# A zero product between the score halves goes, one w_val group is cut in two, and three output products run in column halves

## The chip, the cores and the metric

The kernel runs on one NeuronCore of a Trainium2 chip. The metric is the device time of one execution in microseconds, lower is better. Before is given as the median of three runs.

## What is computed

Sliding-window attention over 8 batches, 8 heads, 576 positions and 64 features per head, followed by a gated feed-forward layer over the 4608 tokens that come out of it:

```python
scores = scale * np.matmul(q, k.transpose(0, 1, 3, 2))
rel = pos[:, None] - pos[None, :]
mask = (rel >= 0) & (rel < 64)
scores = np.where(mask, scores, -1000000000.0)
...                                              # softmax over the last axis
attn_out = np.matmul(attn, v)
x = attn_out.transpose(0, 2, 1, 3).reshape(B * S, H * D)     # 4608 x 512
gate = np.maximum(x @ w_gate, 0.0)               # 512 x 1536
val = x @ w_val                                  # 512 x 1536
out = (gate * val) @ w_out                       # 1536 x 512
```

Inputs and output are fp32. The kernel computes in fp16 with fp32 sums in PSUM.

## The kernel before

**Tokens and tiles.** Attention is done in units of 192 positions of one batch (names `u_...`), three to a batch, with all heads; heads lie in two halves `hh` of four. Two units make one token tile of 384 columns for the feed-forward part; there are four such tiles (`t` = 0 to 3) and then six of 512 (attention for these is done in quads, `q_...` and `t_...`). In the feed-forward part the 1536 hidden features are 12 blocks of 128, numbered `f`.

**The order of work.** The program is written out by hand and fixed when it is built. `tc.manual_schedule()` keeps the instructions of each engine in the order in which the Python code emits them. A small event queue, `Weaver` (`W`), interleaves side work with the long stream of matrix products: `W.at(t, fn)` queues a function for a planned time, and the code that emits products moves the planned clock `W.clock` on and pops what is due. Semaphores between engines are set by the tile framework from what each instruction reads and writes.

**The start.** The first queries and keys come in by DMA; VectorE (DVE) and ScalarE (ACT) cast them to fp16, and DVE transposes them (`qk_trans`, L199), keys and queries of the first head half, then of the second. Meanwhile TensorE (PE) writes a mask bias into eight PSUM banks (`bias_mm`, L243). Then follow, in PE's order: the scores of units 0 and 1 for the first head half (`u_st`, `st_block`, L276), the same for the second half, the values (`u_pv`, L347) of unit 0, and of unit 1. ACT takes exponentials of the scores (`u_exp`, L310), one call for each unit, bank and head half, and the values need them. DVE and ACT divide by the row sums (`u_recip` L361, `u_norm` L368, `u_norm_act` L380), and DVE transposes the result into `xt` (`u_turn`, L390), which the feed-forward part reads.

**Products on zeros.** At three places of the start the code emits `keep_hot`: one fp32 product of 128 rows of zeros (`zero32`) by 384 columns, added to a PSUM bank that holds something else, so that no value changes. An fp32 product shows in the trace as a pair of PE instructions at L240. The first comes behind the bias products, the second between the two score halves, the third between the values of unit 0 and unit 1. `heat` (L237) is a similar fp16 product.

**Feed-forward, tile 0 and 1.** `first_hidden` (L638, L643) makes the hidden blocks f = 0 to 3 of tile 0, `hidden` (L605) the blocks 4 to 11 and tile 1. For a group of four blocks, `hidden` first makes the w_gate products (ACT takes the maximum with zero), then the w_val products (DVE multiplies the two into `g_sb`, L586). Each block has four products, over four chunks `c` of the 512 inputs; a weight load of 256 KB brings chunks 0 and 1 of four blocks, another one chunks 2 and 3. The argument `halves` says how many blocks of a group are interleaved by halves: chunks 0 and 1 of each of them first, then chunks 2 and 3 of each.

**Output of tile 0.** `output(0, (0, 1, 2), (0, 4, 8, NF))` makes three 128-row groups `sub` of the output, over f = 0 to 3, then 4 to 7, then 8 to 11, in three PSUM banks; `out_mm` (L1100) emits one product of 512 columns for each `sub` and f, or, for some f, two of 256 columns.

**The rest.** Tiles 2 to 9 use a scheme with seven products instead of eight for 2 x 2 blocks (`fast_hidden`, L709; `SevenOut`, L922; `fast_output`, L842). The change does not touch it.

Of the kernel before, what the change touches and what calls it, by code (L numbers as in the profile page):

```python
# [47 lines left out]
def kernel(  # L48
# [12 lines left out]
    DM = H * D  # L61
    DF = moe_w_gate.shape[1]
    NT = B * S
    U = 192
# [3 lines left out]
    NF = DF // 128  # L68
    G = 4
    scale = 1.0 / float(D) ** 0.5  # L70
    TT = 2 * U
# [70 lines left out]
    units = {}  # L142
# [3 lines left out]
    def xt_tile(t):  # L146
        if t not in xts:
            xts[t] = x_sb.tile([128, NC, WT], FP16, name="xt")
        return xts[t]
# [14 lines left out]
    def w_need(wt, f, a=1):  # L164
        while (wt.name, f, a) not in w_done:
            W.pop()
        W.advance(w_done[wt.name, f, a])
# [55 lines left out]
    def v_first(copy, other):  # L223

        t = v16s[0]
        copy(t[64:128, 0, :, 0:64], t[0:64, 1, :, 0:64])
        copy(t[0:64, 2, :, 0:64], t[64:128, 1, :, 0:64])
        for hh in range(2):
            h = slice(G * hh, G * hh + G)
            copy(t[64:128, 2, h, 0:64], t[0:64, 3, h, 0:64])  # L230
        copy(t[0:64, 4, :, 0:64], t[64:128, 3, :, 0:64])
        other(t[64:128, 4, :, 0:64], t[0:64, 5, :, 0:64])
# [6 lines left out]
    def keep_hot(to):  # L239
        nc.tensor.matmul(to, zero32[:, 0:128], zero32[:, 0:to.shape[1]], start=False, stop=False, skip_group_check=True)  # L240
# [6 lines left out]
    def one_bank():  # L247
        taken["one"] += 1
        to = singles[(taken["one"] - 1) % 4]
        while id(to) in unread:  # L250
            W.pop()
        return to
# [41 lines left out]
    def u_st(u, hhs=(0, 1)):  # L294
        d = units.setdefault(u, {})
        if "st" not in d:
            st_tiles(u)
        run_rows([[st_block(d["st"][g][:, U * hh + 64 * w:U * hh + 64 * w + 64], g, hh, UB * u + w, "biased" in d)
                   for hh in hhs for w in range(UB)] for g in range(G)])
        return 0.29 * len(hhs)  # L300
# [4 lines left out]
    def u_exp(u, i, hhs=(0, 1)):  # L305
        d = units[u]
        if d["p"][i] is None:
            d["p"][i] = a_p.tile([128, 2 * UB, 64], FP16, name="p", tag="p")
        h0, h1 = hhs[0], hhs[-1] + 1
        nc.scalar.activation(d["p"][i][:, UB * h0:UB * h1].rearrange("p n c -> p (n c)"),  # L310
                             d["st"][i][:, U * h0:U * h1], ACT.Exp, scale=scale)
        if u == 7:
            read(d["st"][i], True)
# [104 lines left out]
    def part_written(banks):  # L418
        written.update((id(to), 0) for to in banks)
# [148 lines left out]
    def hidden(t, spans, f0=0, f1=NF, each=1, halves={}, split=(), banks=None):  # L568

        if t not in gs:  # L570
            gs[t] = g_sb_p.tile([128, NF, WT], FP16, name="g_sb"), {}
        g_sb, done = gs[t]
        xt = xt_tile(t)
        n = spans[0][1] - spans[0][0]

        w = 512 // n
        each = max(each, w)

        def part(tile):
            return tile[:, 0:w * n].rearrange("p (w n) -> p w n", w=w)  # L580

        def relu(r_sb, h1):
            nc.scalar.activation(part(r_sb), part(h1), ACT.Relu)

        def gate(f, c0, r_sb, h2):
            nc.vector.tensor_tensor(g_sb[:, f:f + w, c0:c0 + n], part(r_sb), part(h2), MUL)  # L586
            done.update(dict.fromkeys(range(f, f + w), c0 + n))

        for fb in range(f0, f1, each):
            r2s = [f_sb.tile([128, 2, WT], FP32, name="pr", bufs=4) for _ in range(2)]  # L590
            r_sbs = {}
            for i, wt in enumerate((wg, wv)):
                items = [(c0, f) for c0, _ in spans for f in range(fb, fb + each, w)]
                first = halves.get((fb, i), 1)
                for group in [items[:first]] + [[item] for item in items[first:]]:
                    hs = [singles[banks.pop(0)] if banks else one_bank() for _ in group]
                    part_written(hs)
                    for cs in ((0, 1), (2, 3)) if len(group) > 1 else (range(NC),):
                        for (c0, f), h in zip(group, hs):
                            for b in range(w):  # L600
                                W.advance(W.clock)
                                w_need(wt, f + b, cs[-1] // 2)
                                m = n // 2 if i == 0 and f in split else n
                                for c, lo in ((c, lo) for c in cs for lo in range(0, n, m)):
                                    nc.tensor.matmul(h[:, b * n + lo:b * n + lo + m], wt[:, c, (f + b) * 128:(f + b) * 128 + 128],  # L605
                                                     xt[:, c, c0 + lo:c0 + lo + m], start=(c == 0 and lo == 0 and not (len(group) > 1 and b)),
                                                     stop=(c == NC - 1), skip_group_check=len(group) > 1 or m < n)
                                W.clock += len(cs) * (n + 7) / 2400.0
                            if cs[-1] < NC - 1:
                                continue  # L610
                            if i == 0:
                                r_sb = r_sbs[c0, f] = r2s[len(r_sbs) // 2][:, len(r_sbs) % 2]
                                W.at(W.clock, lambda r_sb=r_sb, h=h: relu(r_sb, h))
                            else:
                                W.at(W.clock, lambda f=f, c0=c0, r_sb=r_sbs[c0, f], h=h: gate(f, c0, r_sb, h))
# [477 lines left out]
    def out_mm(t, op, sub, f):  # L1093
        g_sb, done = gs[t]
        while done.get(f, 0) < sub * 128 + 128:
            W.pop()
        w_need(wo, f)
        n = DM // 2 if t == 0 and NF - 1 > f >= 9 else DM
        for lo in range(0, DM, n):
            nc.tensor.matmul(op[:, lo:lo + n], g_sb[:, f, bass.ds(sub * 128, 128)], wo[:, f, lo:lo + n],  # L1100
                             start=(f == 0 and lo == 0), stop=(f == NF - 1), skip_group_check=n < DM)
        W.clock += 519 / 2400.0
# [20 lines left out]
    def output(t, subs=None, cuts=(0, NF)):  # L1123
        ops = {}
        subs = range(widths[t] // 128) if subs is None else subs
        for group in [[sub] for sub in subs] if len(cuts) == 2 else [subs]:
            for f0, f1 in zip(cuts, cuts[1:]):
                for sub in group:
                    if f0 == 0:
                        ops[sub] = op_tile()  # L1130
                    for f in range(f0, f1):
                        if f % 4 == 0:
                            W.advance(W.clock)
                        out_mm(t, ops[sub], sub, f)
                    if f1 == NF:
                        out_evac(t, ops[sub], sub)
# [15 lines left out]
    with tc.manual_schedule():  # L1152
# [33 lines left out]
        for hh in range(2):  # L1186
            for u in range(2):
                u_st(u, (hh,))
                for i in range(G):
                    u_exp(u, i, (hh,))  # L1190
            if hh == 0:
                keep_hot(units[0]["st"][0][:, 0:2 * U])
        v_first(dve, pool)
        for hh in range(2):
            u_pv(0, (hh,), True)
# [133 lines left out]

        W.advance(15.3)  # L1330
        first_hidden()
        hidden(0, ((0, TT),), 4, NF, 4, split=(4, 5), halves={(8, 0): 3, (8, 1): 3})
        hidden(1, ((0, U),), each=4, banks=[0, 1, 4, 5, 2, 3, 0, 1, 2, 3, 0, 1])
        taken["one"] += 2
        output(0, (0, 1, 2), (0, 4, 8, NF))
# [78 lines left out]
```

## Time and profile before

| what | value |
|---|---|
| time, median of 3 runs | 300.97 us (300.88 to 301.49) |
| profiled execution, its own time | 300.85 us |
| span of the profiled execution, first to last instruction | 299.2 us |
| TensorE (PE) busy | 289.9 us, 97% |
| weight loads (PEld) busy | 240.3 us, 80% |
| VectorE (DVE) busy | 251.5 us, 84% |
| ScalarE (ACT) busy | 197.0 us, 66% |
| GpSimd (POOL) busy | 200.8 us, 67% |

The profile is one execution. Its times count from the first instruction of the span; the profiled execution's own time has 1.7 us more than the span. A view of the timeline gives for each merged group its start, its length, the engine, the line of the kernel, the operation, what is written and read, the shape and how many; brackets give idle time of the engine just before and what ended it. Matmuls are pipelined: one of 384 columns is shown with a length that reaches over the start of the next, so the distance of starts is what PE spends on it. The chain of waits starts at the last instruction and goes back at each step to what released it.

### The profile page before, as it was taken

To read this page: it belongs to the slowest core of one execution; us is meant where nothing else is said; L and a number is where in the kernel's file an instruction comes from. 1 tells how busy PE (TensorE), PEld (TensorE's weight loads), DVE (VectorE), ACT (ScalarE), POOL (GpSimd) and SP (SyncE) were. 2 spreads that over 40 slices of the span, in tenths; PEclk is the share of its full clock that TensorE was granted. 3 is DMA by queue.
4 is the path that set the end of the run, shared out by engine and by line. 5 is a ranking of instruction groups with operands and counts; after the bars stand their busy time and mean duration, and the time that the engine had idled before them with its cause. 6 is when DMAs were issued, how large, how long until landed. Compare 5 with 4: busy or idle time off the path is not lost.

```text
span 299.2 us, 11099 instructions
## 1 busy us (share of the span) xinstructions
PE 289.9 (97%) x4657; PEld 240.3 (80%) x4657; DVE 251.5 (84%) x513; ACT 197.0 (66%) x410; POOL 200.8 (67%) x240
## 2 busy tenths in 40 slices
PE   4899999999999999999999999999999999999994
PEld 2486867949958966888888888888888888888894
DVE  5948886998995999779999899989858985896584
ACT  3745236358848847984798579857985798538850
POOL 8767799858967883985958595759375617441750
PEclk9999999999999999999999999999999999999999
DMA  7999999989919636921399139922911210021013
GB/s 216 184 197 202 194 192 163 213 138 204 81 41 193 162 79 134 133 54 37 65 218 123 54 54 221 127 56 57 181 27 34 77 38 0 3 99 46 1 37 105
DMA packets 59506, 33.20 MB, mean 111 GB/s; under 512 B 39552, under 2 KB 53824, under 8 KB 59456
## 3 DMA queue, kind: packets, MB, share of 16 engines
q0 software_dynamic: 46688, 18.29, 52.6%
q1 hardware_dynamic: 12192, 13.75, 15.3%
q8 instruction: 36, 0.59, 0.8%
q10 hardware_dynamic: 576, 0.46, 0.5%
q14 instruction: 14, 0.11, 0.1%
HBM read 37.75 MB, written 9.44 MB: 158 GB/s over the span
## 4 chain that ended last, share of the span: by engine, by line
PE 96%; DVE 1%; POOL 1%; issue 0%; ACT 0%; DVEq 0%; POOLq 0%
PE bank L709 46%; PE bank L922 18%; PE bank L605 9%; PE bank L842 5%; PE bank L1100 5%; PE bank L276 4%; PE bank L476 3%; PE bank L347 1%; PE bank L643 1%; PE bank L240 1%; PE bank L243 1%; PE bank L638 0%; POOL nats L179 0%; ACT p L310 0%; DVE pr L1088 0%
## 5 line engine op out<-in xcount | busy, mean ns | idle before, releaser
L734 POOL TENSOR_TENSOR g_sb<-pr 128x512 f16<-128x512 f32 (+1 forms) x36 | 42.7, 1191 | 42.5 <-ACT pr L751 42.5
L745 DVE TENSOR_TENSOR pr<-bank,pr 128x512 f32<-128x512 f32 (+1 forms) x96 | 58.5, 650 | 3.6 <-PE bank L709 1.9
L728 ACT COPY pr<-bank 128x512 f32<-128x512 f32 (+1 forms) x96 | 49.1, 566 | 13.6 <-PE bank L709 13.5
L734 DVE TENSOR_TENSOR g_sb<-r,bank 128x512 f16<-128x512 f32 (+1 forms) x48 | 31.3, 652 | 22.8 <-ACT r L778 22.2
L922 PEld LDWEIGHTS <-g_sb 128*128 128x128 f16 x444 | 41.8, 98 | 5.0
L709 PE MATMUL bank<-xc,us 128*128 128x256 f16 (+2 forms) x292 | 41.3, 265 | 0.0
L709 PE MATMUL bank<-xc,vs 128*128 128x256 f16 (+2 forms) x292 | 41.3, 265 | 0.0
L709 PEld LDWEIGHTS <-vs 128*128 128x128 f16 x388 | 36.6, 98 | 3.5
L709 PEld LDWEIGHTS <-us 128*128 128x128 f16 x388 | 36.6, 98 | 3.2
L205 POOL DMA_DIRECT2D v<-in_v_dram x41 | 34.7, 869 | 1.9 <-DMA nats<-in_q_dram 1.1
L751 ACT ACTIVATE pr<-pr 128x512 f32<-128x512 f32 (+1 forms) x48 | 29.3, 610 | 9.8 <-DVE pr L745 9.8
L778 ACT ACTIVATE r<-bank 128x512 f32<-128x512 f32 (+1 forms) x48 | 27.7, 577 | 4.8 <-PE bank L709 4.0
L709 PEld LDWEIGHTS <-wg 128*128 128x128 f16 x288 | 27.4, 98 | 3.2
L709 PEld LDWEIGHTS <-wv 128*128 128x128 f16 x288 | 27.4, 98 | 2.6
L709 PE MATMUL bank<-xt,wv 128*128 128x256 f16 (+1 forms) x192 | 27.5, 266 | 0.0
L709 PE MATMUL bank<-xt,wg 128*128 128x256 f16 (+1 forms) x192 | 27.5, 266 | 0.0
L872 POOL TENSOR_TENSOR g_sb<-g_sb,xus 128x512 f16<-128x512 f16 x24 | 27.0, 1144 | 0.0
L922 PE MATMUL bank<-wo,g_sb 128*128 128x256 f16 (+1 forms) x222 | 26.6, 270 | 0.0
L441 ACT ACTIVATE pw<-bank 128x512 f16<-128x512 f32 x48 | 25.3, 606 | 1.1 <-PE bank L276 0.7
L922 PE MATMUL bank<-wts,g_sb 128*128 128x256 f16 (+1 forms) x222 | 25.6, 270 | 0.0
L718 ACT COPY bank<-bank 128x512 f32<-128x512 f32 (+1 forms) x48 | 24.5, 552 | 0.0
L310 ACT ACTIVATE p<-bank 128x384 f16<-128x384 f32 (+1 forms) x40 | 14.1, 442 | 10.1 <-PE bank L276 9.8
(120 smaller groups left out, 558.4 us busy)
## 6 DMA issues: line engine op xcount, KB each, us to landing
out_dram<-o_sb SPq DMA_DIRECT2D x30, 256.0 KB, 3.3
nats<-in_k_dram POOLq DMA_DIRECT2D x15, 288.0 KB, 5.5
nats<-in_q_dram POOLq DMA_DIRECT2D x15, 288.0 KB, 7.9
v<-in_v_dram POOLq DMA_DIRECT2D x31, 128.0 KB, 7.7
v<-v SPq DMA_DIRECT2D x27, 66.0 KB, 2.8
v<-v SPq DMA_DIRECT2D x13, 132.0 KB, 2.4
wg<-in_moe_w_gate_dram POOLq DMA_DIRECT2D x6, 256.0 KB, 6.9
wv<-in_moe_w_val_dram POOLq DMA_DIRECT2D x6, 256.0 KB, 8.3
```

Of the source, the lines that this page charges most:

```text
L205: nc.gpsimd.dma_start(v16s[b % 2][lo:hi, g, :, 0:64], v[b, :, 64 * g - 64 + lo:64 * g - 64 + hi].rearrange("h p d -> p h d"))
L441: nc.scalar.activation(d["p"][g].rearrange("p n c -> p (n c)"), d["st"][g], ACT.Exp, scale=scale)
L605: nc.tensor.matmul(h[:, b * n + lo:b * n + lo + m], wt[:, c, (f + b) * 128:(f + b) * 128 + 128], xt[:, c, c0 + lo:c0 + lo + m], start=(c = ...
L709: nc.tensor.matmul(to[:, HT * m + lo:HT * m + lo + step], w[:, k, 128 * m:128 * m + 128], x[:, k, lo:lo + step], start=(first and m == 0 a ...
L718: nc.scalar.copy(at[j, "B", i][:, 0:TW], at[j, "A", i][:, 0:TW])
L728: nc.scalar.copy(pr[:, i], at[j, "A", i][:, 0:TW])
L734: eng.tensor_tensor(gh[:, f:f + 2, h], pair(r), pair(v), MUL)
L745: nc.vector.tensor_tensor(pr[:, i], to[:, 0:TW], pr[:, i], ADD)
L751: nc.scalar.activation(pr[:, 0], pr[:, 0], ACT.Relu)
L778: nc.scalar.activation(r, to[:, 0:TW], ACT.Relu)
L872: eng.tensor_tensor(to, x, y, op)
L922: nc.tensor.matmul(at[key][:, QN * m * whole:QN * m * whole + n1 - n0], A[:, 128 * m:128 * m + 128], B[:, c, n0:n1], start=(first and m == ...
```

## The change

One place where a zero product is emitted goes: the second of the three, behind the first head half's scores. In the last group of w_val blocks of tile 0 (f = 8 to 11) two blocks instead of three are interleaved by halves; the third is then made in one go, as the fourth is already. In the output of tile 0 the products of f = 8 are made in two column halves, as those of f = 9 and 10 are already, which is one product for each of the three row groups.

```diff
@@ out_mm
-        n = DM // 2 if t == 0 and NF - 1 > f >= 9 else DM
+        n = DM // 2 if t == 0 and NF - 1 > f >= 8 else DM
         for lo in range(0, DM, n):
             nc.tensor.matmul(op[:, lo:lo + n], g_sb[:, f, bass.ds(sub * 128, 128)], wo[:, f, lo:lo + n],
                              start=(f == 0 and lo == 0), stop=(f == NF - 1), skip_group_check=n < DM)
@@ the start
                 u_st(u, (hh,))
                 for i in range(G):
                     u_exp(u, i, (hh,))
-            if hh == 0:
-                keep_hot(units[0]["st"][0][:, 0:2 * U])
         v_first(dve, pool)
@@ tile 0
-        hidden(0, ((0, TT),), 4, NF, 4, split=(4, 5), halves={(8, 0): 3, (8, 1): 3})
+        hidden(0, ((0, TT),), 4, NF, 4, split=(4, 5), halves={(8, 0): 3, (8, 1): 2})
```

In PE's order this takes out one fp32 product on zeros, moves two w_val products of f = 10 (chunks 0 and 1) behind the four products of f = 8 and f = 9 on chunks 2 and 3, and puts six products of 256 columns, each with its weight load, in the place of three of 512. The order of instructions on DVE, ACT, POOL and SP is the same as before.

## The prediction

> **What bounds the kernel now.** I read the page first: which engine carries the chain that ended last.
>
> ```profile
> span 299.2 us, 11099 instructions
> PE 289.9 (97%) x4657; PEld 240.3 (80%) x4657; DVE 251.5 (84%) x513; ACT 197.0 (66%) x410; POOL 200.8 (67%) x240
> ...
> PE 96%; DVE 1%; POOL 1%; issue 0%; ACT 0%; DVEq 0%; POOLq 0%
> ```
>
> TensorE is the end's path. The chain of waits in order of time has, from 15.02 to 294.03 us, one piece that is not PE (0.07 us of "issue" at 16.96). So a delay that reaches PE's work at 15 us reaches the end whole, and a step that is not on PE costs nothing later. What is left to move lies before 15.02 us. There the chain reads:
>
> ```profile
> 9.24 1.28 PE bank L240 x2
> 10.52 0.39 PE bank L276 x18
> 10.91 0.33 ACT p L310
> ...
> 12.30 0.84 PE bank L240 x2
> 13.15 0.43 PE bank L347 x39
> 13.58 0.20 DVE r L361
> ...
> 14.48 0.50 DVE xt L390
> 14.98 0.04 issue
> 15.02 0.49 PE bank L643 x4
> 15.51 1.45 PE bank L638 x8
> ```
>
> The removed pair is the first line, 1.28 us, and it looks like a free gain. The timeline of all engines from 0 to 17 us (start, length, instruction, in brackets the idle time and who ended it) says what stands behind it:
>
> ```profile
> 4.39 2.72 PE L243 MATMUL bank<-bias,ident 128*128 128x384 f16 x8 [4.39 <-DVE bias L129]
> 6.91 1.48 PE L240 MATMUL bank<-wts 128*128 128x384 f32 x2
> 8.34 0.83 PE L276 MATMUL bank<-qT,kT 32*128 32x64 f16 x48
> 8.86 1.89 ACT L310 ACTIVATE p<-bank 128x192 f16<-128x192 f32 x8 [2.11 <-PE bank L276]
> 9.21 1.24 DVE L199 STREAM_TRANSPOSE qT<-nats 128x576 f32<-128x576 f32 x1
> 9.24 1.28 PE L240 MATMUL bank<-wts 128*128 128x384 f32 x2
> 10.45 0.56 PEld L276 LDWEIGHTS <-kT 32*128 32x128 f16 x48 [0.71 <-DVE qT L199]
> 10.50 0.64 PE L276 MATMUL bank<-qT,kT 32*128 32x64 f16 x48
> 15.48 1.47 PE L638 MATMUL bank<-xt,wg 128*128 128x384 f16 x8
> ```
>
> Two things are to be seen. The weight load of the second score half was released at 10.45 by DVE's transpose of q (9.21 + 1.24), which the pair does not touch. And the clock: 8 matmuls of 384 columns take 2.72 us at 4.39 and 1.47 us at 15.48, some 320 ns apart against 163. PE starts at half speed. The trace's record of the granted clock begins at 10.01 us, with full clock; narrow windows of the same timeline show the removed pair's two parts starting at 9.24 and 10.03, so 0.79 us for the first, at half clock. The clock rose inside the pair that goes.
>
> **The change part by part.** *The pair.* Direct gain: scores start when DVE is done, about 0.02 us after the weight load as at 8.32/8.34, so at 10.47 for 10.50. That is 0.03 us, not 1.28. ACT is idle for 0.15 us before its second eight exponentials (the first eight end at 10.75, the next start at 10.90), so the 0.03 us passes to the values, to DVE and to 15.02.
>
> *What the pair did for the clock.* No trace of the kernel without it exists, so I bound it. Lower end: the clock rises at 10.01 all the same, +0. Against that: PE was busy for 4.77 of the 4.85 us from 4.39 to 9.24, and at 9.24 still had half clock (the 0.79 us). That work alone had not brought the rise by then, and without the pair a pause of 1.5 us (8.93 to 10.47) follows. Other end: the pause wipes the account, and the rise needs again the 5.62 us from first matmul to rise (4.39 to 10.01), counted from 10.47: 16.1 us. I take this end, as the nearest measured stretch of activity that was followed by a rise. Half clock until 16.1 costs, along the chain:
> - First exponential of the second half: 0.52 us after its first score at half clock (8.34 to 8.86), 0.40 at full (10.50 to 10.90): 10.47 + 0.52 = 10.99, +0.09. ACT runs the eight back to back, so the values of unit 0, which wait for the fourth, are late by 0.09.
> - Values after that exponential, 24 small matmuls: 48 scores took 0.83 against 0.64, so half of 0.19: +0.10.
> - The zero pair at 12.23, which stays: 0.84 in the chain at full clock; at half 0.79 + 0.64 (the pair at 6.91: 1.48 less a tail of 0.20, halved) = 1.43: +0.59.
> - 48 values of unit 1: +0.19.
> Sum 0.97. Reciprocal, norm and transpose on DVE (13.58 to 14.98) follow PE, so w_gate's first products start at 15.99 for 15.02. Four of 192 columns lie partly before 16.1: +0.04. L638 behind them waits for DVE's next transpose, late by the same 0.97. From there all is PE: **+1.0 us** at the end. The later w_gate and w_val loads are paced by DMA and would only gain room.
>
> The Trainium skill, page "TensorE: Matmul & The Clock Gate", section "Part 1: The HAM clock gate", has the clock doubled only after a busy window of 3413 ns on a fixed raster. The trace agrees: full clock is on record for 290.13 us, 85.0 such windows. With edges at 6.60 and 10.01 the deciding window was busy about 86% with the pair (pauses of 0.15 us before the scores and 0.31 after) and would be about 63% without; the window before, 65% busy (from 4.39 on), did not raise the clock. By that rule the rise moves to 13.43 or, as 10.01 to 13.43 would be about 65% busy too, to 16.84, and the sum would be +1.3 us.
>
> *Column halves of f = 8.* Three products of 512 columns (one for each of three 128-row groups of tile 0) become six of 256, with three more weight loads. 17 matmuls from 47.25 to 49.65 us are 12 of 256 and 5 of 512 columns; 512 columns run 0.216 us apart (0.110 x 2 = 0.220 for the two halves): +0.004 each, +0.01 in all. The added loads (98 ns each) run under the matmul before.
>
> *w_val group 8.* Two w_val matmuls of f = 10 (0.163 us each) move behind four of f = 8 and 9. PE's work is the same, and the 16 matmuls run from 29.43 to 32.03 without a gap. f = 8 and 9 end 0.33 us earlier, so their gates on DVE may, which nobody waits for: g_sb is first read at 40.7. The price could be a wait for the second half of w_val: its load is issued at 20.43 and lands 8.8 us later at most (the slowest of six), 29.2; its weight load moves from about 30.25 to 29.92. Room of 0.7 us, so nothing; with the cover gone it would be PE's wait, one for one. The order of instructions on DVE, ACT, POOL and SP does not change, so no queue is passed.
>
> Sum: 1.0 - 0.03 (already in the 10.47) + 0.01: +1.0. Profiled execution 300.85 us (span 299.2 and 1.7 around it) gives 301.85, the median of the runs shown, 300.97, gives **302.0**.
>
> **Rivals.** *A, nothing moves (not slower).* The clock has risen before the second scores anyway. For it: rise need not follow work at once, and this is one execution. The price is the gain of 0.03 less 0.01: 300.95. It decides if the clock is full by 10.5. The same page (Part 1, "What's actually happening") says the raster runs freely and does not reset with the kernel. As a mechanism here: if the position of the rise is drawn anew in each run, the clock would often be full by 9 us, before the pair, and then only runs whose rise fell inside the pair or just after it (9.5 to 10.5) lose, fewer than half, and the median stays at 300.95. Against: before's three runs and its profile lie within 0.6 us, which a free rise also gives, since the pair covers any rise up to 10.5. So the times don't separate these. By that raster the rise came 3.00 windows after -0.23 us, just ahead of the first instruction, weak evidence that it starts with the program.
>
> *B, half way.* The clock comes back near 13.4, inside the zero pair that stays. Its price: 0.09 + 0.10 and, of the pair's 0.59, about 0.4, the unit 1 values at full clock: +0.55, 301.5.
>
> *C2, later still.* The clock stays at half through L638: 8 x 0.163 more and four 192-column products: +2.4, 303.4. It needs the work from 12.3 to 16 not to count, which is nearly gapless; little chance.
>
> *D, faster.* By over 0.6 us nothing in the trace allows it: ahead of 15.02 the path without PE (DMA, transposes, exponentials) gives back 0.03. I leave a little for what one trace doesn't show.
>
> **Numbers.** The clock lost until about 16 us 0.50, A 0.24, B 0.12, C2 0.08, D 0.06. 0.2% is 0.6 us, about the spread of before's runs (300.88 to 301.49) and what a measurement can tell from no change. Slower by more: the first and C2, 0.58; within: A and B, 0.36; faster 0.06. The range takes in A below and reaches above to the main case with the w_gate products still at half clock (+1.6): 300.8 to 302.6; C2 and D stay outside. The main case's own range is 301.8 to 302.6.
>
> **What would show it.** Right: in the profile after, the zero pair (now at about 12.4) lasts about 1.4 us instead of 0.84, the first L643 after DVE's transpose starts near 16.0 instead of 15.02, and from L605 on every PE pitch is as before. Second scores still start within 0.05 of 10.47. Wrong: the pair at 12.2 still takes 0.84 and the 15.02 start stays (A); or the start is right but the end isn't later by the same amount, so that PE had slack I deny; or a PE gap appears at 29.9 before w_val's second half.

## The result: slower by 0.3%, and the profile after

The changed kernel takes 301.88 us (median of 8 runs, 301.45 to 302.24) where before takes 300.93 (8 runs, 300.73 to 301.49). The ratio is 1.0028, 95% interval 1.0019 to 1.0038: +0.95 us, for +1.0 forecast. The profiled execution of the changed kernel is the quickest of its eight, 301.45 us, against 300.85 for the one of before, so its trace shows 0.60 us of loss. Ratios here and below are of runs that were not disturbed on the chip, with 95% intervals, and are not quotients of the medians.

The page, for the lines shown of before, and its row of the granted clock in 40 slices of 7.5 us:

```profile
span 299.8 us, 11101 instructions
...
PE 289.8 (97%) x4658; PEld 240.7 (80%) x4658; DVE 251.0 (84%) x513; ACT 197.0 (66%) x410; POOL 200.7 (67%) x240
...
PEclk9899999999999999999999999999999999999999
...
PE 93%; DVE 4%; DMA 1%; ACT 1%; issue 0%; DVEq 0%
```

```text
(before, the same row)  PEclk9999999999999999999999999999999999999999
```

PE has as much to do as before and the span is 0.6 us longer. What is new is the 8 in the second slice, 7.5 to 15 us: the granted clock was not full there. Three windows of the trace of the changed kernel show it (stretch, its length, then busy time and number of instructions for PE, PEld, DVE, ACT and POOL, the granted clock, and two figures on DMA):

```profile
9.28:12.69 3.41, 1.99 (x98) 1.51 (x98) 3.25 (x11) 3.26 (x15) 1.77 (x4) 1.00 1.78 174
12.69:16.10 3.41, 3.30 (x59) 1.88 (x58) 2.37 (x7) 2.72 (x13) 3.41 (x6) 0.50 1.24 205
16.10:18.00 1.90, 1.90 (x17) 1.38 (x16) 0.49 (x1) 1.17 (x3) 1.90 (x3) 1.00 1.24 204
```

The clock was full by 9.28 us, went back to half for 3.41 us from 12.69 to 16.10, and was full from then on. In the stretch ahead of the half one PE was busy for 1.99 of 3.41 us. The chain of waits of the same trace shows where the half clock falls:

```profile
9.38 1.09 DVE qT L199
10.47 0.05 issue
10.52 0.41 PE bank L276 x23
10.93 0.33 ACT p L310
...
12.33 1.18 PE bank L240 x2
13.51 0.81 PE bank L347 x36
...
14.41 0.19 DVE r L361
...
15.04 0.49 DVE xt L390
15.54 0.04 issue
15.58 0.73 PE bank L643 x4
16.31 1.30 PE bank L638 x8
```

DVE's transpose of q now stands in the chain where the pair was, and the second scores still start at 10.52 (10.50 before): the 1.28 us of the pair were hidden. The third zero pair, the values of unit 1 and the first w_gate products lie in the half stretch: 1.18 for 0.84, 0.81 for 0.43, and products 0.16 us apart for 0.08.

### The profile page after: what moved, and what is told of

Same layout as the page of the kernel before. It is cut to its first block, busy times and chain, and to the rows that moved or that the text cites. A ratio compares the mean times of both kernels' runs of the same rounds, so it can differ in the third digit from the quotient of the medians.

```text
span 299.8 us, 11101 instructions
## 1 busy us (share of the span) xinstructions
PE 289.8 (97%) x4658; PEld 240.7 (80%) x4658; DVE 251.0 (84%) x513; ACT 197.0 (66%) x410; POOL 200.7 (67%) x240
## 4 chain that ended last, share of the span: by engine, by line
PE 93%; DVE 4%; DMA 1%; ACT 1%; issue 0%; DVEq 0%
PE bank L709 46%; PE bank L922 18%; PE bank L605 8%; PE bank L842 5%; PE bank L1100 5%; PE bank L276 4%; PE bank L476 3%; PE bank L347 2%; PE bank L643 1%; DMA vs<-in_k_dram 1%; DVE qT L199 1%; DVE kT L199 1%; DVE p L317 1%; PE bank L638 0%; PE bank L240 0%; DVE g_sb L586 0%
## 5 line engine op out<-in xcount | busy, mean ns | idle before, releaser
L922 PEld LDWEIGHTS <-g_sb 128*128 128x128 f16 x444 | 41.8, 98 | 5.0
L922 PE MATMUL bank<-wo,g_sb 128*128 128x256 f16 (+1 forms) x222 | 26.6, 270 | 0.0
L922 PE MATMUL bank<-wts,g_sb 128*128 128x256 f16 (+1 forms) x222 | 25.6, 270 | 0.0
```

The lines of the kernel that those rows point to most:

```text
L922: nc.tensor.matmul(at[key][:, QN * m * whole:QN * m * whole + n1 - n0], A[:, 128 * m:128 * m + 128], B[:, c, n0:n1], start=(first and m == ...
```

## Experiments

Each ran against before on the same chip; ratios are to before's runs there. Where a median is given for before, it is of those runs.

**1. The two parts of the change alone.**

```diff
 e1, against before
-            if hh == 0:
-                keep_hot(units[0]["st"][0][:, 0:2 * U])
 e2, against before
-        n = DM // 2 if t == 0 and NF - 1 > f >= 9 else DM
+        n = DM // 2 if t == 0 and NF - 1 > f >= 8 else DM
-        hidden(..., halves={(8, 0): 3, (8, 1): 3})
+        hidden(..., halves={(8, 0): 3, (8, 1): 2})
```

> Only the zero pair between the score halves is taken out; w_val group and column halves stay as before. Theory (the pair kept TensorE's clock, by filling the pause of 1.6 us between the score halves): the whole loss is here, 301.9 us (301.6 to 302.2), some half clock between 10 and 17 us in the profile. Rival (the w_val order or the halved products cost it): 300.9, as before.

> The pair stays; w_val group 8 with two blocks by halves, and f = 8 in column halves. Theory: 300.9 us, +0.01 by the rows, full clock from about 10 us or earlier to the end. Rival: over 301.4, with a PE gap near 30 or 47 to 50 us.

Without the pair: 301.94 us for 300.75, ratio 1.0030 (1.0017 to 1.0043). With the pair and the other two edits: 300.86, ratio 0.9997 (0.9982 to 1.0013). So the pair accounts for the loss, and the time of the rest can't be told from nothing (the interval allows 0.5 us of gain or 0.4 of loss). e1's own trace has full clock from 9.61 us and half clock from 13.02 to 16.43. In e2's timeline the last w_val group and the halved products are as priced:

```profile
29.20 2.76 PE L605 MATMUL bank<-xt,wv 128*128 128x384 f16 x16
31.80 1.40 PE L605 MATMUL bank<-xt,wg 128*128 128x192 f16 x15
...
46.87 2.57 PE L1100 MATMUL bank<-wo,g_sb 128*128 128x256 f16 x19
49.28 0.82 PE L605 MATMUL bank<-xt,wg 128*128 128x192 f16 x8
```

The w_val group takes 2.60 us from its first start to the next line's (29.43 to 32.03 before, 2.60), so nothing waits for w_val's second half; the three row groups' last part takes 2.41 us for 2.40. One small gain does show between them: the 48 scores at L276 that start at 38.07 in before take 0.62 us to the next product, 0.63 in e1 (39.27 to 39.90), and 0.48 in e2 (37.83 to 38.31), as in the changed kernel (38.66 to 39.14). Every trace with the new w_val order is the same here, so that order seems to be worth about 0.14 us; which wait went, the profile does not show.

The mean granted clock of each run bears on the cause. A half-clock stretch of 3.41 us in some 293 us of record makes it 0.994. Of e1's twelve runs ten have 0.994 or less; of the 29 runs of before beside them one has (302.45 us, the slowest), the others 0.997 to 1.000 (e2's trace has 0.997 by a clock that falls at 297.26, 2.5 us after PE's last product starts).

**2. What fills the pause.**

```diff
 e3, against after: ahead of v_first(dve, pool), in the loop over hh
+            if hh == 0:
+                for _ in range(3):
+                    nc.tensor.matmul(units[0]["st"][0], zero[:, 0:128], zero[:, 0:512], start=False, stop=False, ...)
 e4, against after, in the same place
+            if hh == 0:
+                for _ in range(28):
+                    for j in range(4):
+                        nc.tensor.matmul(units[0]["st"][0][32 * j:32 * j + 32, 0:65], zero[:, 0:32], zero[:, 0:65], ...)
```

> The changed kernel with three fp16 products on zeros of 512 columns at the place of the fp32 pair (3 x 0.43 us at half clock, the same 1.3 us). Theory (what counts is that PE works in the pause): 300.9 us, as before. Rival (something of the fp32 product itself, its four passes or its two weight loads): 301.9, as after.

> The changed kernel with 112 small products on zeros at the place of the pair, in the form of the values (32 output rows, 65 columns, four column groups beside each other), about 1.3 us at half clock. If any PE work counts for the clock: 300.9 us. If only products that fill the array do: 301.9, with the clock at half for a stretch between 10 and 17 us as after.

Three fp16 products do what the fp32 pair does: 301.04 us, ratio 0.9996 (0.9982 to 1.0009), full clock from 7.21 us to the end of its trace. Nothing of fp32 is needed. The small products were a miss: 308.08 us, ratio 1.0240 (1.0205 to 1.0275), worse than both expectations. Its timeline shows that the products did more than fill:

```profile
12.62 0.27 PE L347 MATMUL bank<-v,p 128*32 128x65 f16 x5
16.26 0.79 PE L347 MATMUL bank<-v,p 128*32 128x65 f16 x43 [3.37 <-issue]
```

PE stood still for 3.4 us with no wait that the profile shows, and full clock is on record only from 20.43 us. Much later PE stood still once more, and there the clock was taken back (a line of the timeline, then two windows with PE's busy time and the clock):

```profile
64.08 0.54 PE L347 MATMUL bank<-v,p 128*32 128x65 f16 x47 [2.35 <-issue]
...
61.39:64.81 3.42, 1.07 (x95) 1.00 1.77 151
64.81:68.22 3.41, 3.41 (x25) 0.50 0.47 48
```

PE had been busy almost without a break for 40 us before that. Whether small products count for the clock is not answered by this run. What the two gaps are is taken up in the last section.

**3. Half a pair.**

```diff
 e5, against after
+            if hh == 0:
+                keep_hot(units[0]["st"][0][:, 0:U])
```

> The changed kernel with a zero pair of half the width (192 columns, 0.64 us at half clock, 0.79 with its weight load) between the score halves: of the pause from 8.95 to 10.5 us, about 0.7 us stays idle. If the clock follows the busy share of a stretch: between the two kernels, 300.9 to 301.5 us, and near 300.9 if a pause of 0.5 us at a time does no harm. If only a full cover helps: 301.9.

301.83 us for 301.19, ratio 1.0016 (0.9998 to 1.0034): as a median inconclusive, but its twelve runs fall apart by clock. Eight have a mean clock of 0.993 or 0.994 and take 301.55 to 303.44 us; four have 0.997 to 1.000 and take 300.60 to 301.10. Half a cover helps in some runs and not in others, by whether the clock was lost. The profiled run is one of the eight:

```profile
7.80:11.10 3.30, 1.45 (x51) 1.00 1.95 167
11.20:14.50 3.30, 3.23 (x98) 0.50 1.35 201
14.60:18.00 3.40, 2.67 (x64) 1.00 1.24 205
```

(PE's busy time and the clock, in windows just inside the three stretches.)

**4. A late rise, or a clock taken back.** The prediction had the clock coming late. The first profile had it coming in time and going again. e7 makes it come early, and leaves the pause; e8 and e11 are the changed kernel again, for two more records.

```diff
 e7, against after
+        heat(4, units[0]["st"][3])
         u_bias(0)
```

> The changed kernel with four fp16 zero products of 512 columns ahead of the bias products, so PE works without a break from about 2.5 to 8.2 us and the clock can rise well before the pause, which stays unfilled. If the loss is a rise that comes late: 300.9 us. If it is a clock that is given and taken back because of the pause: 301.4 to 301.9, and the record of the clock shows full, half for about 3.4 us between 12 and 16, full.

> The changed kernel once more, for a second record of the clock: either the rise comes late (full clock on record only from 12.7 us or later), or it is taken back for 3.4 us as in its first profile. Time 301.4 to 302.3 us in both.

> The changed kernel a third time, for its record of the clock. Theory (given and taken back): full, half for 3.4 us, full, with the half stretch between 9 and 17 us. The other pattern, which two of the first records did not show: a rise that only comes at 11 to 14 us and stays.

e7 takes 301.70 us for 301.19, ratio 1.0025 (1.0014 to 1.0036), and all twelve of its runs have a clock of 0.994 or less. PE's windows in e7's trace, then in e8's and e11's:

```profile
7.20:10.50 3.30, 1.17 (x50) 1.00 1.94 167
10.60:17.30 6.70, 6.46 (x156) 0.50 1.28 196
17.40:20.00 2.60, 2.60 (x27) 1.00 1.24 205
```

```profile
7.70:11.00 3.30, 1.36 (x98) 1.00 2.10 156
11.10:14.40 3.30, 3.06 (x81) 0.50 1.21 193
14.50:18.00 3.50, 2.79 (x50) 1.00 1.24 205
```

```profile
8.50:11.80 3.30, 1.48 (x123) 1.00 2.06 166
11.90:15.20 3.30, 3.28 (x74) 0.50 1.24 207
15.30:18.00 2.70, 2.31 (x19) 1.00 1.24 204
```

In all three the clock is given and taken back. e8 takes 301.81 us, e11 301.96. The stretch ahead of the loss held 1.17 to 1.55 us of PE work in 3.30 (e7, e8, e11, e5, e1), 1.99 of 3.41 in the first profile. In the traces that kept the clock through the start, the first 3.41 us at full clock held 2.01 (e3) to 3.24 us (before). So for these records the cause is the pause itself, read at the end of the stretch in which it lies; 1.99 and 2.01 lie too close together to be read as a threshold. Three of the first eight runs of the changed kernel have a clock of 0.992 or 0.994; the other five have 1.000 and are no quicker (301.77 to 302.24). Since the record starts with the first full clock, a rise that comes late would look like that. There is no trace of such a run, so that second pattern is argued, not shown.

**5. The early products with the pair kept.**

```diff
 e9, against after
+        heat(4, units[0]["st"][3])
         u_bias(0)
...
+            if hh == 0:
+                keep_hot(units[0]["st"][0][:, 0:2 * U])
```

> The four early zero products of e7, and the zero pair between the score halves kept; w_val order and column halves as after. Theory (e7 lost because the pause took the clock back): 300.8 us, as before, with full clock from about 7 us to the end. Rival (the early products do harm of their own): 301.7, as e7.

A miss: 301.49 us for 300.90, ratio 1.0013 (1.0001 to 1.0025). The clock does what the theory says, it is full from 6.66 us until PE is done, and still 0.4 us by the ratio, 0.6 by the medians, are lost. Its trace, of a run of 301.82 us, has this gap:

```profile
15.62 0.82 PE L638 MATMUL bank<-xt,wg 128*128 128x384 f16 x4
17.05 0.81 PE L638 MATMUL bank<-xt,wg 128*128 128x384 f16 x4 [0.60 <-issue]
```

The product at 17.05 starts 0.76 us later than the pace of its neighbours; in before the like gap at 17.03 is 0.23. Another 0.41 us go at 27.58, where a product of L605 waits for DVE's `g_sb`; e3, e8 and e12 have that wait too, so it doesn't come from the early products alone. So the times of e7 and e9 don't separate the theories; their traces do, since e7 has the half clock and not the gap at 17 us, and e9 the gap and no half clock.

**6. Two pairs.**

```diff
 e6, against after
+            if hh == 0:
+                keep_hot(units[0]["st"][0][:, 0:2 * U])
+                keep_hot(units[0]["st"][0][:, 0:2 * U])
```

> Two zero pairs between the score halves, w_val order and column halves as after. PE then reaches the second scores at 11.2 to 11.8 us instead of 10.5, with the clock up in time. If a delay of PE there reaches the end whole: +0.65 to +1.3, 301.5 to 302.2 us, with full clock through. If there is slack between the scores and the first w_gate products: 300.9.

301.55 us for 301.19, ratio 1.0012 (0.9998 to 1.0025): inconclusive, and less of a loss than expected. In its trace the clock is full from 7.86 us and the pairs run from 9.74 to 11.23; in e5's trace, where the first inputs came as late (first scores at 9.05 and 8.95), the second scores waited for DVE until 11.21. At full clock two pairs fit into the pause too, so this run doesn't measure what a delay there costs.

**7. The third pair taken out.** The table in the next section shows that at half clock most of the loss is the longer third pair, so its own cost was tried.

```diff
 e10 and e12, against e2
-        keep_hot(units[0]["st"][3][:, 0:2 * U])
         u_recip(0, (0,))
```

> The pair between the score halves kept, the zero pair between the values of unit 0 and unit 1 taken out; w_val order and column halves as after. That pair is 0.84 us of PE's path, so the values of unit 1 come up to 0.5 us earlier; DVE's last transpose (15.46 to 16.04) then waits for ACT and lets at most 0.2 us through: 300.6 to 300.8 us if the clock stays full. If this pair, too, holds the clock: 301.5 or more, with half clock for 3.4 us on record.

> The kernel of e10 once more (pair between the score halves kept, the third zero pair out), to narrow its interval: if its 0.2 to 0.3 us are real, the ratio to before is again 0.9985 to 0.9995; if they were chance, within 0.0005 of 1.

300.65 us for 300.90, ratio 0.9990 (0.9980 to 1.0001); again 300.69 for 301.14, 0.9990 (0.9980 to 1.0000). The clock stays full from 7.68 us until PE is done in e10's trace. It is quicker than the changed kernel, and against before it gains 0.1%, at the edge of what these runs can tell, by the way that was expected:

```profile
13.35 0.49 PE L643 MATMUL bank<-xt,wg 128*128 128x192 f16 x4
14.80 0.49 PE L643 MATMUL bank<-xt,wg 128*128 128x192 f16 x4 [0.95 <-DVE xt L390]
15.26 1.57 PE L638 MATMUL bank<-xt,wg 128*128 128x384 f16 x8
```

The values end earlier and the first w_gate products behind DVE's transpose start at 14.80 for 15.02.

## Why the prediction was right, and where its steps were not

**The direct gain is nothing: right.** Second scores start at 10.52, 10.57 and 10.49 us in the three traces of the changed kernel, for 10.47 forecast and 10.50 before. DVE's transpose ends the wait.

**The clock is lost: right; how it is lost: wrong.** The step "the pause wipes the account, and the rise needs again the 5.62 us" failed for every run of the changed kernel that has a trace. In the three traces the clock is full at 9.28, 7.64 and 8.46 us, before the pause is over, and half clock comes later, for 3.41 us, from 12.69, 11.06 and 11.87. The stretch of half clock that the prediction laid from the start to 16.1 us ends there in one trace by chance; in the others at 14.47 and 15.29. For the five of the first eight runs with a mean clock of 1.000 it stays open whether the step held.

**The price: right in sum, in part by luck, and not in its terms.** From the chains and timelines, in us:

| step | before | forecast | first profile | e8 |
|---|---|---|---|---|
| first exponential of the second half | 10.91 | 10.99 | 10.93 | 10.98 |
| values of unit 0, to the third pair | 1.02 | 1.12 | 1.03 | 1.19 |
| third zero pair, length in the chain | 0.84 | 1.43 | 1.18 | 1.58 |
| values of unit 1, length in the chain | 0.43 | 0.62 | 0.81 | 0.57 |
| w_gate product behind DVE's transpose | 15.02 | 15.99 | 15.58 | 16.13 |
| first w_val product | 17.68 | 1.0 later | 18.10 | 18.56 |
| profiled execution | 300.85 | 301.85 | 301.45 | 301.81 |

The scores still had full clock, so they lost nothing; the exponentials are late by 0.02 and 0.07 because the scores started that much later. The third pair's +0.59 lies between +0.34 and +0.74, the +0.19 for the values of unit 1 between +0.38 and +0.14. What each lost depends on where the half stretch falls, and so does the time. In the first profile DVE takes up 0.2 us of it: its chain has one reciprocal behind the values, before's has two.

By the first w_val product the loss is 0.42 us in the first profile, 0.88 in e8 and 0.86 in e11. What ends as 0.60, 0.96 and 1.11 us of time has later steps in it that the prediction put at nothing. The largest are 0.22 us near 27 us in e8, where L605 waits for DVE's `g_sb`, 0.46 us at 57.4 in e11, and 0.14 us the other way at 38 in all three. Runs of before with a mean clock of 0.997 or more reach from 300.49 to 301.96 us themselves. That the median comes out at +0.95 for +1.0 is therefore closer than the terms deserve.

**PE has no slack behind 15 us: nearly.** In before's trace the L643 product at 17.03 starts 0.39 us after its predecessor, where 0.16 us is the rule; the prediction passed over this as 0.07 us of "issue". The loss of 1.11 us at 16.13 in e8 is 0.88 at the first w_val product (18.56 for 17.68), since that gap is not there.

**Rival A, the raster.** The free raster is what the traces show: the rise falls at 7.64 to 9.28 us in the same kernel, so the "weak evidence that it starts with the program" was chance. But A's consequence, fewer than half of the runs lose, is wrong: every run of the changed kernel took at least 301.45 us, because a clock that has risen is taken back as well. The page "TensorE: Matmul & The Clock Gate" of the Trainium skill, Part 1, has the raster free and its window 3413 ns, and the trace agrees (the half stretch lasts 3.413 us in six records, those of the first profile, e1, e4, e5, e8 and e11, and 6.827 in e7's). Its section "Why this matters for your kernels" asks for no idle gaps over about 3 us; here a pause of 1.3 to 2.0 us was enough, and the measurement decides. Of the window up to 10.01 the prediction took 86% as busy, by pauses of 0.15 and 0.31 us; the view of windows counts 3.34 of its 3.41 us.

**The other two edits: right within what e2 can tell.** Their price of +0.01 us is far inside its interval. The prediction counted no gain from the w_val order, though, and the scores at 38 us show 0.14 us of it.

**Rivals B and C2.** No record of the changed kernel shows the late rise that they rest on. In e7 the half clock lasted two stretches, 6.8 us, although PE was busy for 6.46 of 6.70 us in it; why one stretch of that didn't bring the clock back stays open. A half stretch with 3.18 us of work brought it back in e8, one with 3.20 did not in e7.

## What to carry to other kernels

A product that stands in the chain with 1.28 us may cost nothing and still be worth 1 us: ask what the engine would do without it, and read the granted clock ahead of and behind it. A pause of about 1.5 us next to a half-idle stretch can cost 3.4 us of half clock, at the start of a kernel as here or later (e4, at 64.8 us), and the loss is what lies on PE's path in that time. Three fp16 products of 512 columns cover it as well as an fp32 pair; cover with few large products, not with many small ones.

## What was not expected of the hardware

**A clock that is given goes again after a pause of 1.3 to 2.0 us.** The stretches followed by half clock held 1.17 to 1.55 us of PE work in 3.30 (e1, e5, e7, e8, e11), 1.99 in 3.41 (the first profile), and 1.07 in e4 at 61 us. At the end of before's trace the clock stayed full until 300.15, 5 us after PE's last product at 295.12; in e11's it fell 2.4 us after, in e4's 5.6. So the length of the pause alone does not decide. Nor does busy time alone: at the end of e8 and e4 stretches with 1.93 and 1.47 us of work, all products of 256 columns at L922, kept the clock, where 1.99 us with many scores and values in them lost it. Small products may count for less; no run tests that by itself.

**PE seems to wait for its own instructions.** The gaps without a wait, in before (0.23 us more than the pace, at 17.03), e9 (0.76, at 17.05), e12 (0.23, at 17.04) and e4 (3.4, at 16.26), all stand ahead of the 450th row of PE's and PEld's instructions in the trace, in order of their starts. Each time the row starts 1.51 to 1.57 us after the first 16 KB packet of the queue marked "instruction" has ended (15.48, 15.48, 15.51 and 14.75 us); in e6 a gap of 0.07 us stands there, 1.39 us after. In e2, where the packet ended at 15.19, the row ran at 16.79 without a gap. Another gap stands ahead of the 1730th row, 5 x 256 further: 0.2 us at 56.9 in the first profile of the changed kernel, 0.5 us at 57.4 in e11. The second gap of e4, 2.35 us at 64.08, stands ahead of the 1986th, 6 x 256 further. So products that are added early bring such a row sooner and can make PE wait: by this reading the 224 rows of e4 by 3.4 us, the 8 of e9 by 0.5 more than before. This was read from the traces and no run was made for it alone.
